# A planned two-part kernel: turns of x move to TensorE, folds stay in float32, and the order of work is planned in eight passes

## The chip, the cores and the metric

The kernel runs on one core of one Trainium2 chip. The metric is the device time of one launch in microseconds. Five engines work side by side: TensorE (PE, with its weight loads listed as PEld), VectorE (DVE), ScalarE (ACT), GpSimd (POOL, almost unused here) and SyncE (SP), which issues the DMAs.

## The reference

Three parts follow one another (B=8, H=8, S=512, 32 state rows, D=64; 4608 tokens in all).

```python
scores = scale * x @ state.T          # per batch and head: 512 x 32
xread  = softmax(scores) @ state      # 512 x 64
sread  = softmax(scores.T) @ x        # 32 x 64
x = concat([xread, sread])            # per batch 544 rows, 8 heads side by side: 512 columns
h = ((x @ w1) * (x @ w2)) @ w3        # w1, w2: 512 x 1024, w3: 1024 x 1024
x = h @ w_out                         # 1024 x 512
h = x @ w_in2                         # 512 x 2048
out = (h - tanh(h)) @ w_out2          # 2048 x 512
```

The weights arrive as 8-byte floats; x and state are 4-byte floats.

## The kernel before, in words

**Numbers.** A weight of 8 bytes is unpacked to float32 by five operations (`unpack_parts`): ACT takes the absolute value of the high word (L261), ACT or DVE scales the low word (L267, L269), DVE clamps (L278), shifts (L283) and joins (L289). For the fast matmul format (float32r) a float32 tile is split in a high and a low half: ACT copies (L220), DVE subtracts (L223), and each product is three matmuls (`PASSES`).

**First part, planned (everything up to `plan.run()`).**
- `w3_turn` turns a block of w3 by four 128x128 transposes on PE (tile `w_ps`, L242), ACT copies it out (`w3t`), and `w3_mul` multiplies it with w_out in float32 (tile `w3o_ps`, L735). There are 16 such turns with their products; the result takes the place of w3 and w_out.
- For each half of the batches (r = 0, 1) `turn_state` turns the state rows on PE (`u_ps`), they are split in halves (`uu`), and `fold` multiplies them with w1 and w2 (tile `m_ps`, L877; six matmuls on 64 rows, two at a time at different row positions). 32 folds go through PSUM and SBUF (`fe`) to DRAM (`mdr`). By them the read of the state and the product with w1 and w2 are one matmul per head.
- `attn_parts(b)`: x of a batch is loaded twice, as `xn` (for sread) and as `xb` (bands of 32 rows, eight DMAs of 128 KB, for the scores). DVE turns `xb` in 32x32 blocks (`xt`, L408, four per batch) and the state (`ut`). `scores` is 16 float32 matmuls on 32 rows and 32 columns (tile `sc_ps`, L421), each of which the trace shows as two records. Then come the two softmaxes, four transposes twice (`et_ps`), and `sread` (`sr_ps`, L516).
- `stage1(b, k, h)` makes the products with w1 and w2 (tile `ab_ps`, L250), `stage2` the product with the joined w3 (tile `y_ps`, L1027), for k = 0 to 7 in each of 9 blocks: 8 batches of 512 rows, and block B, the 256 state rows of all batches, which takes w1 and w2 themselves (tile `w`, split in halves at decode).
- w_in2 and w_out2 are decoded and stored to DRAM meanwhile.

**Second part, in a fixed order.** `stage3` (tile `h_ps`, L250), `curve`, `stage4` (tile `o_ps`, L1286) and `finish` for the 9 blocks.

**What sets the order of the first part.** Every operation is a `part` with an engine, a duration from a small cost table, what it needs, makes, takes and gives back. Parts lie in streams; each stream has a rank for each engine. `Plan.run` walks once: it takes the part that can start first and, among the parts of the same engine that can start within 250 ns of it, the one of the lowest rank. The order so found is the program order on each engine's queue. Four PSUM banks are shared by `ab`, `w3x`, `fold` and `ps` tiles, the others hold the accumulators. The turns of w3, their copies and the products `w3_mul` lie in one stream, one after the other.

## Time and profile before

| what | us |
|---|---|
| runs | 1343.75, 1333.1, 1341.79 (median 1341.79) |
| the profiled execution | 1337.37 |
| its span, first to last instruction | 1335.5 |
| PE busy in the span | 1282.8 (96%) |
| DVE busy | 978.2 (73%) |
| ACT busy | 723.9 (54%) |

Busy times are sums over an engine's instructions, overlaps counted once. The ends of matmuls are modelled, so PE's busy time holds part of its waits too. In the rows below a group of instructions shows its count as xN, then the busy time in us and the mean ns of one; a timeline row shows the start, the length from first start to last end, the engine, the line, and in brackets how long the engine stood idle before and what ended that.

### The profile page before, as it was taken

Reading aid. Unit: us, or ns where it says so; the run is one execution under the profiler, and the core shown is the slowest. Engines: PE = TensorE matmul, PEld = TensorE weight load, DVE = VectorE, ACT = ScalarE, POOL = GpSimd, SP = SyncE. Lnnn points to the kernel's source line nnn. Section 1 sums busy time; section 2 is a strip of 40 time slices with the busy share of each in tenths; the row PEclk is TensorE's granted clock in tenths of the full one; section 3 lists DMA queues with packets and bytes.
Section 4 is the critical chain, followed back from the end, with each engine's and each line's share of the span. In section 5 each row is a group of like instructions: output and inputs, shape, how many; then the busy total and the mean of one; then the engine's idle time right before and its main releaser. Section 6 shows DMA issues by size and latency. Waiting matters only on the chain.

```text
span 1335.5 us, 17513 instructions
## 1 busy us (share of the span) xinstructions
PE 1282.8 (96%) x6416; PEld 1005.6 (75%) x6416; DVE 978.2 (73%) x1638; ACT 723.9 (54%) x1172; POOL 0.7 (0%) x6
## 2 busy tenths in 40 slices
PE   6798999999999999999999999999999999999996
PEld 3345676767777689788888888888888888888886
DVE  7898786775655842559977687787876877768775
ACT  7788575564646622446555455454544545545454
POOL 0000000000000000000000000000000000000000
PEclk9999999999999999999999999999999999999999
DMA  9966887869899632722010010100101001001000
GB/s 326 270 226 212 255 256 214 246 200 280 250 250 284 189 91 95 220 69 90 1 64 1 9 56 0 64 0 1 64 0 54 10 1 64 1 0 48 1 32 16
DMA packets 98286, 150.58 MB, mean 113 GB/s; under 512 B 13976, under 2 KB 68248, under 8 KB 96152
## 3 DMA queue, kind: packets, MB, share of 16 engines
q1 hardware_dynamic: 98200, 149.46, 36.2%
q8 instruction: 51, 0.84, 0.3%
q14 instruction: 35, 0.29, 0.1%
HBM read 98.04 MB, written 51.38 MB: 112 GB/s over the span
## 4 chain that ended last, share of the span: by engine, by line
PE 73%; DMA 12%; DVE 5%; ACT 4%; SPq 4%; issue 1%; DVEq 0%; ACTq 0%
PE h_ps L250 26%; PE o_ps L1286 26%; PE ab_ps L250 9%; PE y_ps L1027 7%; DMA raw_w<-in_moe_w_in_dram 3%; DMA m<-mdr 2%; DMA raw_p<-in_moe_w_dram 2%; PE w3o_ps L735 2%; DMA raw_w<-in_moe_w_out_dram 1%; DMA mdr<-fe 1%; SPq L396 1%; SPq L974 1%; PE m_ps L877 1%; DMA raw_p<-in_moe_w_out_dram 1%; ACT raw L267 1%
## 5 line engine op out<-in xcount | busy, mean ns | idle before, releaser
L250 PE MATMUL h_ps<-yt,w2in 128*128 128x512 f32 (+1 forms) x1728 | 394.0, 377 | 0.0
L250 PEld LDWEIGHTS h_ps<-yt,w2in 128*128 128x128 f32 x1728 | 313.4, 188 | 61.1
L250 PE MATMUL ab_ps<-at,m 128*128 128x512 f32 x768 | 196.2, 404 | 14.1 <-ACT ac L220 4.2
L1027 PE MATMUL y_ps<-ph,w3o 128*128 128x512 f32 (+1 forms) x864 | 201.4, 381 | 3.0 <-ACT y L220 3.0
L250 PEld LDWEIGHTS ab_ps<-at,m 128*128 128x128 f32 x768 | 141.6, 191 | 60.0 <-ACT ac L220 13.9
L1027 PEld LDWEIGHTS y_ps<-ph,w3o 128*128 128x128 f32 x864 | 153.7, 188 | 39.4 <-issue 6.1
L223 DVE TENSOR_TENSOR ph<-ac,ph 128x512 fp32r<-128x512 f32 (+1 forms) x72 | 47.5, 660 | 85.8 <-ACT ph L220 84.8
L220 ACT ACTIVATE ph<-ac 128x512 fp32r<-128x512 f32 (+1 forms) x72 | 43.9, 610 | 104.6 <-PE y_ps L1027 91.7
L735 PE MATMUL w3o_ps<-wo,w3t 128*128 128x512 f32 x128 | 64.0, 646 | 12.6 <-ACT w3t L220 12.6
L735 PEld LDWEIGHTS w3o_ps<-wo,w3t 128*128 128x128 f32 x128 | 24.7, 203 | 43.0 <-issue 26.5
L1010 DVE TENSOR_TENSOR ac<-ab_ps,ac 128x512 f32<-128x512 f32 (+1 forms) x72 | 47.2, 655 | 4.7 <-PE ab_ps L250 4.5
L267 ACT ACTIVATE raw_w<-raw_w 128x512 uint16<-128x512 uint32 x32 | 43.6, 1362 | 0.6
L220 ACT ACTIVATE ac<-ab_ps 128x512 f32<-128x512 f32 (+1 forms) x72 | 40.4, 561 | 2.0 <-PE ab_ps L250 1.9
L1296 DVE COPY ob<-o_ps 128x512 f32<-128x512 f32 x17 | 11.8, 692 | 39.1 <-PE o_ps L1286 39.1
L261 ACT ACTIVATE dt_w<-raw_w 128x512 f32<-128x512 f32 x32 | 21.4, 668 | 32.0 <-DMA raw_w<-in_moe_w_in_dram 16.6
L223 DVE TENSOR_TENSOR m<-m 128x512 fp32r<-128x512 f32 x32 | 22.0, 688 | 22.3 <-ACT m L220 22.0
L220 ACT ACTIVATE fe<-m_ps 128x512 fp32r<-128x512 f32 (+1 forms) x48 | 28.1, 601 | 16.8 <-PE m_ps L877 7.6
L220 ACT ACTIVATE m<-m 128x512 fp32r<-128x512 f32 x32 | 20.2, 631 | 30.2 <-DMA m<-mdr 30.0
L220 ACT ACTIVATE ob<-o_ps 128x512 f32<-128x512 f32 x17 | 10.2, 599 | 45.0 <-PE o_ps L1286 45.0
L877 PE MATMUL m_ps<-w,uu 64*128 64x512 f32 x192 | 32.3, 427 | 2.0 <-DVE fe L900 1.2
L278 DVE TENSOR_SCALAR dt_w<-dt_w 128x512 f32<-128x512 f32 x32 | 13.4, 420 | 23.4 <-ACT dt_w L261 23.2
L877 PEld LDWEIGHTS m_ps<-w,uu 64*128 64x128 f32 x192 | 16.8, 184 | 16.8 <-issue 6.2
(1814 smaller groups left out, 2297.1 us busy)
## 6 DMA issues: line engine op xcount, KB each, us to landing
mdr<-fe SPq DMA_DIRECT2D x96, 256.0 KB, 3.2
m<-mdr SPq DMA_DIRECT2D x128, 128.0 KB, 4.6
xb<-in_x_dram SPq DMA_DIRECT2D x64, 128.0 KB, 3.6
raw<-in_moe_w_dram SPq DMA_DIRECT2D x16, 512.0 KB, 7.3
xn<-in_x_dram SPq DMA_DIRECT2D x8, 1024.0 KB, 6.4
m<-mdr SPq DMA_DIRECT2D x128, 64.0 KB, 2.7
raw_w<-in_moe_w_in_dram SPq DMA_DIRECT2D x16, 512.0 KB, 5.9
raw_w<-in_moe_w_out_dram SPq DMA_DIRECT2D x16, 512.0 KB, 5.5
```

The costliest lines, as they stand in the source:

```text
L220: nc.scalar.activation(dst, src, AF.Copy)
L223: nc.vector.tensor_tensor(out=lo, in0=src, in1=hi.bitcast(F32), op=ALU.subtract)
L250: nc.tensor.matmul(out_ap, lhs(i), rhs(j), start=(n == 0), stop=(n == m - 1))
L261: nc.scalar.activation(t.bitcast(F32), w[:, :, 1].bitcast(F32), AF.Abs)
L267: nc.scalar.activation(tail, w[:, :, 0], AF.Copy, scale=TAIL)
L278: nc.vector.tensor_scalar(out=t, in0=t, scalar1=EXP_LO, scalar2=EXP_HI, op0=ALU.max, op1=ALU.min)
L396: nc.sync.dma_start(xb[b][band(q, j), j].rearrange("p g c d -> p g (c d)"), x[b, 2 * q + j].rearrange("(g p c) d -> p g (c d)", p=NS, c=NC),)
L735: nc.tensor.matmul(acc[a], v[:, a * P:(a + 1) * P], wo[j][:, 512:].bitcast(F32), start=(j == 0), stop=(j == nj - 1),)
L877: nc.tensor.matmul(ts[j].rearrange("p (k f) -> p k f", k=2), uu[r][1][d, i, q * P:(q + 1) * P], w[d, :, l, q, :], start=(n == 0), stop=(n ...
L1010: nc.vector.tensor_tensor(out=ab[b, k], in0=ab[b, k, 1], in1=ab[b, k], op=ALU.mult)
L1027: nc.tensor.matmul(acc[o][:, :n], w3o[k // 4][:, k // 2 % 2, i, c + o * P:c + (o + 1) * P], p[:, j], start=(k == 0 and e == 0), stop=(k == ...
L1286: nc.tensor.matmul(acc[t], g[:, i, t * P:(t + 1) * P], w[:, l, c], start=(f == 0 and e == 0), stop=(f == NF - 1 and e == 2),)
```

## The change

- **x is loaded once and turned by PE.** `xb`, `load_xb`, the DVE transposes and the second copy of the state (`zb`, `ut`) are gone. `xn` is loaded by four DMAs of 256 KB with runs of 256 bytes, in two buffers. Four times per batch PE makes four 128x128 transposes (`turn_x`) and ACT copies the bank to `xt`.
- **Scores on 64 rows.** Eight float32 matmuls on 64 rows and 32 columns.
- **Float32 folds.** w1 and w2 are no longer split at decode: a block is unpacked in one piece of 1024 instead of two of 512, in place, and a fold is two float32 matmuls on 64 rows instead of six float32r ones. `uu` stays float32.
- **Late halves.** Block B takes its halves of w1 and w2 when it needs them (`own_hi` on ACT, `own_lo` on DVE), in the ring `m` that the other blocks' weights use.
- **Turns of w3 as an own stream**, ahead of the products in rank.
- **State rows row by row.** The columns of `xsr` go by row and batch, and so do the last two stores.
- **The plan is made eight times.** The first pass is the walk by ranks. After each pass `justify` goes backwards over the plan and finds for each part the latest start that would not move the end; these take the place of the ranks in the next pass. The pass with the earliest planned end of PE is kept.

```diff
             can = []
-            for s in self.streams:
+            for s, parts in zip(self.streams, lists):
                 seen = set()
-                for k, p in enumerate(s["parts"][:s["ahead"]]):
+                for k, p in enumerate(parts[:s["ahead"]]):
                     if p["eng"] not in seen:
                         seen.add(p["eng"])
                         t = self.start(p)
                         if t is not None:
-                            rank = s["rank"].get(p["eng"], 9) if p["rank"] is None else p["rank"]
-                            can.append((t, rank, s["parts"], k, p))
+                            can.append((t, p["late"], parts, k, p))
             if not can:
-                left = [s["parts"][0] for s in self.streams if s["parts"]]
+                left = [parts[0] for parts in lists if parts]
                 assert not left, [(p["eng"], p["need"], p["take"]) for p in left]
-                return
             t0, _, _, _, p0 = min(can, key=lambda c: c[0])
             t, _, parts, k, p = min(
                 (c for c in can if c[4]["eng"] == p0["eng"] and c[0] <= t0 + self.NEAR),
                 key=lambda c: (c[1], c[0]),
             )
             del parts[k]
-            self.emit(p, t)
+            self.place(p, t)
+            found.append(p)
+        return found
...
+    def justify(self, found):
+
+        end = max(p["span"][1] for p in found)
+        gaps = {e: [(0.0, end)] for e in self.REACH}
+        bound = {id(p): end for p in found}
+        for s in self.streams:
+            last = {}
+            for p in s["parts"]:
+                if p["eng"] in last:
+                    p["after"].append(last[p["eng"]])
+                last[p["eng"]] = p
+        late = {}
+        for p in sorted(found, key=lambda p: -p["span"][1]):
+            free = gaps[p["eng"]]
+            k = next(
+                (
+                    k for k in reversed(range(len(free)))
+                    if min(free[k][1], bound[id(p)]) - free[k][0] >= p["dur"]
+                ),
+                0,
+            )
+            a, b = free[k]
+            t = min(b, bound[id(p)]) - p["dur"]
+            free[k:k + 1] = [(a, t), (t + p["dur"], b)]
+            late[id(p)] = t
+            for q in p["after"]:
+                lag = q["lag"] if q["eng"] != p["eng"] or q["bytes"] else 0.0
+                bound[id(q)] = min(bound[id(q)], t - lag)
+        for p in found:
+            p["late"] = late[id(p)]
+
+    def run(self):
+        for s in self.streams:
+            for p in s["parts"]:
+                p["late"] = s["rank"].get(p["eng"], 9) if p["rank"] is None else p["rank"]
+        best = None
+        for _ in range(self.ROUNDS):
+            found = self.order()
+            end = max(p["span"][1] for p in found if p["eng"] == "PE")
+            if best is None or end < best[0]:
+                best = end, [(p, p["banks"]) for p in found]
+            self.justify(found)
+        for p, banks in best[1]:
+            self.picked += banks
+            p["fn"]()
...
-            uu[r] = (t, pt.tile([P, 2, 512], F32R, tag="uu", name=f"uu{r}"))
+            uu[r] = (t, pt.tile([P, 512], F32, tag="uu", name=f"uu{r}", bufs=2))
...
+                t = pt.tile([P, NC, H, D], F32, tag="xn", name=f"xn{b}", bufs=2)
+                xn[b] = t.rearrange("p c h d -> p c (h d)")
+                for c in range(NC):
+                    nc.sync.dma_start(
+                        t[:, c], x[b].rearrange("h (p c) d -> c p h d", c=NC)[c]
+                    )
...
-            def xt(j, e):
-                t = pt.tile([P, 512], F32, tag="xt", name=f"xt{b}_{j}{e}", bufs=4)
-                nc.vector.transpose(
-                    out=t.rearrange("p (c g i) -> p g c i", c=NC, g=4),
-                    in_=xb[b][:, j, :, :, e * NS:(e + 1) * NS],
-                )
-                s["xt", j, e] = t
+            def turn_x(q):
+                s["xp", q] = ps(f"x_ps{b}_{q}")
+                transposes(s["xp", q], [xn[b][:, c, q * P:(q + 1) * P] for c in range(NC)])
+
+            def xt(q):
+                s["xt", q] = pt.tile([P, 512], F32, tag="xt", name=f"xt{b}_{q}", bufs=4)
+                copy(s["xt", q], s["xp", q])
 
             def scores():
                 for j in range(G):
                     s["ps", j] = ps(f"sc_ps{b}_{j}")
-                for e in range(2):
-                    for q in range(KT):
-                        for j in range(G):
-                            d = band(q, j)
-                            nc.tensor.matmul(
-                                s["ps", j][q * NS:(q + 1) * NS],
-                                ut[b // 4][d, j, bb, e], s["xt", j, e][d],
-                                start=(e == 0), stop=(e == 1), tile_position=(d.start, q * NS),
-                            )
+                for q in range(KT):
+                    for j in range(G):
+                        d = slice(j * D, (j + 1) * D)
+                        c = q * P + bb * NS
+                        nc.tensor.matmul(
+                            s["ps", j][q * NS:(q + 1) * NS], uu[b // 4][1][d, c:c + NS],
+                            s["xt", q][d], start=True, stop=True, tile_position=(d.start, q * NS),
+                        )
...
-                    xsr[:, :, b * NS:(b + 1) * NS],
+                    xsr.rearrange("p q (n b) -> p q n b", b=B)[:, :, :, b],
...
+                    "PE", pe_t(4), turn_x, (q,), [("xn",)], [("xp", q)], [("ps", ("xp", q), 1)],
+                    [("xn",)],
+                )
+                p(
+                    "ACT", ("scalar", 512), xt, (q,), [("xp", q)], [("xt", q)],
+                    [("xt", ("xt", q), 1)], [("xp", q)],
                 )
             part(
-                a_s, "PE", 16 * 185, scores,
-                [("ut", b // 4)] + [(b, "xt", j, e) for j in range(G) for e in range(2)],
+                a_s, "PE", 1300, scores, [("uu", b // 4)] + [(b, "xt", q) for q in range(KT)],
...
+        t3_s = plan.stream({"PE": 2.8, "ACT": 1.5, "DVE": 1.5}, 40)
...
-                x_s, "PE", 4 * TURN, later(w3_turn, t), whole[:1], [("w3x", t)],
+                t3_s, "PE", 4 * TURN, later(w3_turn, t), whole[:1], [("w3x", t)],
...
-                x_s, "ACT", ("scalar", 512), lambda t=t: copy(w3v[t], w3x[t]),
+                t3_s, "ACT", ("scalar", 512), lambda t=t: copy(w3v[t], w3x[t]),
...
-        for kk in range(NK // 2):
-            for u in range(4):
-                k = 2 * kk + u // 2
-                unpack_parts(
-                    d_s, ("t12", kk, u), lambda kk=kk, u=u: raws["w12", kk][:, u // 2, u % 2],
-                    lambda kk=kk, u=u: w12_float(kk, u), 512, [("raw12", k, u % 2)],
-                    [("raw", ("t12", k), 4)] if u % 2 == 0 else (), (),
-                )
-            for u in range(4):
-                k = 2 * kk + u // 2
-                part(
-                    d_s, "ACT", ("scalar", 512), lambda kk=kk, u=u: copy(*w12_slice(kk, u)[1::-1]),
-                    [("t12", kk, v) for v in range(4)], [("h12", kk, u)], (), [("t12", k)],
-                )
-                part(
-                    d_s, "DVE", ("vector", 512), lambda kk=kk, u=u: low(*w12_slice(kk, u)),
-                    [("h12", kk, u)], [("w12", kk, u)], (), [("t12", k)],
-                )
+        for k in range(NK):
+            unpack_parts(
+                d_s, ("t12", k),
+                lambda k=k: raws["w12", k // 2][:, k % 2].rearrange("p h f -> p (h f)"),
+                lambda k=k: w12_float(k), 1024, [("raw12", k, h) for h in range(2)],
+                [("raw", ("t12", k))], [("t12", k)], end=lambda k=k: w12_whole(k),
+            )
...
-            w = w12[kk].rearrange("p k l (a f) -> p k l a f", a=KT)
+            w = w12_rows(kk)
             ts = fts[r, kk, q] = [ps(f"m_ps{r}_{kk}_{q}_{j}") for j in range(G)]
-            for n, (i, l) in enumerate(PASSES):
-                for j in range(G):
-                    d = slice(j * D, (j + 1) * D)
-                    nc.tensor.matmul(
-                        ts[j].rearrange("p (k f) -> p k f", k=2),
-                        uu[r][1][d, i, q * P:(q + 1) * P], w[d, :, l, q, :],
-                        start=(n == 0), stop=(n == len(PASSES) - 1), tile_position=(j * D, 0),
-                    )
+            for j in range(G):
+                d = slice(j * D, (j + 1) * D)
+                nc.tensor.matmul(
+                    ts[j].rearrange("p (k h f) -> p k h f", k=2, h=2),
+                    uu[r][1][d, q * P:(q + 1) * P], w[d, :, :, q],
+                    start=True, stop=True, tile_position=(j * D, 0),
+                )
...
+        def own_hi(k, h):
+            mt[B, k, h] = pa.tile([P, 2, 512], F32R, tag="m", name=f"m{B}_{k}{h}", bufs=3)
+            w = w12_rows(k // 2)[:, k % 2, h]
+            copy(mt[B, k, h][:, 0].rearrange("p (a f) -> p a f", a=KT), w)
+
+        def own_lo(k, h):
+            w = w12_rows(k // 2)[:, k % 2, h]
+            m = mt[B, k, h].rearrange("p l (a f) -> p l a f", a=KT)
+            low(w, m[:, 0], m[:, 1])
...
+                for h in range(2):
+                    part(
+                        m_s, "ACT", ("scalar", 512), later(own_hi, k, h),
+                        ["pa", ("s1", *steps[max(0, steps.index(z) - 2)], h)], [("mh", b, k, h)],
+                        [("m", ("m", b, k, h))],
+                    )
+                    part(
+                        m_s, "DVE", ("vector", 512), later(own_lo, k, h), [("mh", b, k, h)],
+                        [("m", b, k, h)],
+                    )
...
-                    ["pa"] + [
+                    ["pa"] + ([("mh", B, NK - 1, 1)] if b == B - 1 else []) + [
...
-                nb = P // NS
+
+                c = S + t * (P // B)
                 nc.sync.dma_start(
-                    out.rearrange("(b s) o -> b s o", b=B)[nb * t:nb * (t + 1), S:], ob[:, t]
+                    out.rearrange("(b s) o -> s b o", b=B)[c:c + P // B], ob[:, t]
```

## Rows read from the trace of the kernel before

**Rows 1.** The page, part 2: busy share of PE in 40 slices of the span, tenths.

```profile
PE   6798999999999999999999999999999999999996
```

**Rows 2.** Windows, busy us of each engine: the first part cut at 112; the second.

```profile
core 0: us, PE busy (x) PEld busy (x) DVE busy (x) ACT busy (x) POOL busy (x), PEclk, DMA share, GB/s
0.00:112.00 112.00, 89.52 (x400) 42.12 (x402) 93.94 (x159) 83.50 (x111) 0.70 (x6) 0.97 0.87 268
112.00:584.00 472.00, 451.83 (x2660) 346.65 (x2661) 298.76 (x559) 253.89 (x429) 0.00 (x0) 0.99 0.70 210
584.00:1335.00 751.00, 741.44 (x3359) 616.87 (x3357) 585.54 (x921) 386.50 (x634) 0.00 (x0) 1.00 0.08 28
```

**Rows 3.** Chain of waits, where the second part begins: start, length, what.

```profile
583.72 10.88 PE h_ps L250 x48
...
597.32 2.72 PE h_ps L250 x12
```

**Rows 4.** Groups on PE, 7 to 584 us; last column: idle before, and releasers.

```profile
L1027 PE MATMUL y_ps<-ph,w3o 128*128 128x512 f32 (+1 forms) x864 | 201.4, 381 | 3.0 <-ACT y L220 3.0
L250 PE MATMUL ab_ps<-at,m 128*128 128x512 f32 x768 | 196.2, 404 | 14.1 <-ACT ac L220 4.2 <-ACT fe L220 2.5 <-DMA raw_w<-in_moe_w_in_dram 1.8
L735 PE MATMUL w3o_ps<-wo,w3t 128*128 128x512 f32 x128 | 64.0, 646 | 12.6 <-ACT w3t L220 12.6
L877 PE MATMUL m_ps<-w,uu 64*128 64x512 f32 x192 | 32.3, 427 | 2.0 <-DVE fe L900 1.2 <-ACT fe L220 0.5 <-ACT w3t L220 0.3
L250 PE MATMUL ab_ps<-atsr,w 128*128 128x256 f32 x192 | 24.3, 284 | 0.1
L421 PE MATMUL sc_ps<-xt,ut 32*32 32x512 f32 x256 | 15.9, 593 | 0.0
L516 PE MATMUL sr_ps<-xn,e2t 128*32 128x64 f32 x512 | 10.1, 222 | 0.3 <-ACT ac L220 0.3
L242 PE MATMUL et_ps<-ident,sc 128*128 128x128 f32 x64 | 9.9, 278 | 1.5 <-ACT sc L446 1.5
```

**Rows 5.** Timeline of PE, the first turn of w3.

```profile
7.25 1.09 PE L242 MATMUL w_ps<-ident,wo 128*128 128x128 f32 x4 [7.25 <-DVE wo L289]
```

**Rows 6.** Timeline of PE, later turns and a product of w3.

```profile
33.65 0.60 PE L242 MATMUL w_ps<-ident,wo 128*128 128x128 f32 x4
34.08 0.60 PE L242 MATMUL u_ps<-ident,zst 128*128 128x128 f32 x4
35.21 3.70 PE L735 MATMUL w3o_ps<-wo,w3t 128*128 128x512 f32 x8 [0.53 <-ACT w3t L220]
38.75 0.60 PE L242 MATMUL w_ps<-ident,wo 128*128 128x128 f32 x4
```

**Rows 7.** Timeline of PE, one set of scores and a fold.

```profile
167.58 1.95 PE L421 MATMUL sc_ps<-xt,ut 32*32 32x512 f32 x32
169.45 0.96 PE L877 MATMUL m_ps<-w,uu 64*128 64x512 f32 x6
170.35 1.65 PE L1027 MATMUL y_ps<-ph,w3o 128*128 128x512 f32 x6
```

**Rows 8.** Groups on DVE, 0 to 112 us.

```profile
L223 DVE TENSOR_TENSOR w<-dt,w 128x512 fp32r<-128x512 f32 x12 | 8.0, 684 | 1.3 <-ACT w L220 1.3
...
L408 DVE STREAM_TRANSPOSE xt<-xb 128x512 f32<-128x512 f32 x8 | 5.3, 692 | 0.0
```

**Rows 9.** Groups on ACT, 0 to 112 us.

```profile
L220 ACT ACTIVATE w3t<-w_ps 128x512 f32<-128x512 f32 x16 | 9.8, 613 | 11.1 <-PE w_ps L242 11.0
```

**Rows 10.** DMA issues: count, KB each, median us to landing.

```profile
xb<-in_x_dram SPq DMA_DIRECT2D x64, 128.0 KB, 3.6
...
xn<-in_x_dram SPq DMA_DIRECT2D x8, 1024.0 KB, 6.4
...
zst<-in_state_dram SPq DMA_DIRECT2D x8, 64.0 KB, 8.4
```

More of the change, by code (lines that the diff above doesn't have):

```diff
@@ L50 @@
     REACH = {"PE": 200.0, "ACT": 130.0, "DVE": 130.0, "SP": 0.0}
+    ROUNDS = 8
     def __init__(self):
-        self.free = dict.fromkeys(self.REACH, 0.0)
-        self.moved = 0.0
-        self.made, self.slots, self.held, self.streams = {}, {}, {}, []
-        self.banks = [([0, 0.0], None) for _ in range(4)]
+        self.rings, self.streams = {}, []
         self.most = {"ab": 4, "w3x": 4, "fold": 2, "ps": 2}
@@ L67, in stream, with clear @@
         return s["parts"]
+    def clear(self):
+        self.free = dict.fromkeys(self.REACH, 0.0)
+        self.moved = 0.0
+        self.made, self.held = {}, {}
+        self.slots = {name: (n, []) for name, n in self.rings.items()}
+        self.banks = [([0, 0.0, []], None) for _ in range(4)]
     def start(self, p):
@@ L93, in start, with place @@
         return t
[L95 removed]
+    def place(self, p, t):
         end = t + p["dur"]
@@ L682, in unpack_parts @@
             part(
-                st, "DVE", ("vector", n), lambda: unpack_end(raw(), t()),
+                st, "DVE", ("vector", n), lambda: unpack_end(raw(), t(), end and end()),
                 [(key, "tail"), (key, "top")], [key], (), give,
@@ L913, in tile_kernel @@
                 f_s, "PE", 4 * TURN, later(turn_state, r), [("zst", r)], [("u_ps", r)],
-                [("fold", ("u_ps", r), 2), ("uu", ("uu", r), KT * NK // 2)], [("zst", r)],
+                [("fold", ("u_ps", r)), ("uu", ("uu", r), KT * NK // 2 + 4)], [("zst", r)],
             )
             part(
-                f_s, "ACT", ("scalar", 512), lambda r=r: copy(uu[r][1][:, 0], uu[r][0]),
-                [("u_ps", r)], [("uh", r)], (), [("u_ps", r)],
-            )
-            part(
-                f_s, "DVE", ("vector", 512),
-                lambda r=r: low(uu[r][0], uu[r][1][:, 0], uu[r][1][:, 1]),
-                [("uh", r)], [("uu", r)], (), [("u_ps", r)],
+                f_s, "ACT", ("scalar", 512), lambda r=r: copy(uu[r][1], uu[r][0]),
+                [("u_ps", r)], [("uu", r)], (), [("u_ps", r)],
             )
@@ L928, in tile_kernel @@
                     part(
-                        f_s, "PE", 6 * 177, later(fold, *f),
-                        [("uu", r)] + [("w12", kk, u) for u in range(4)], [("fold", *f)],
+                        f_s, "PE", 1080, later(fold, *f),
+                        [("uu", r)] + [("t12", 2 * kk + k) for k in range(2)], [("fold", *f)],
                         [("fold", ("m_ps", *f, j), 2 if r else 1) for j in range(G)], [("uu", r)],
@@ L961, in tile_kernel @@
         steps = [(b, k) for b in blocks for k in range(NK)]
-        m_s = plan.stream({"SP": 0})
+        m_s = plan.stream({"SP": 0, "ACT": 1, "DVE": 1})
         n_s = plan.stream({"ACT": 1, "DVE": 1})
@@ L1067, in tile_kernel @@
             else:
+                for h in range(2):
[8 more added lines that the diff above has]
+                    )
                 need = [(B - 1, "atsr", q) for q in range(0, KT, 2)]
-                need += [("w12", k // 2, u) for u in range(4)]
                 used, dur = [(B - 1, "atsr")], 12 * 120
@@ L1072, in tile_kernel @@
                 part(
-                    s1, "PE", dur, later(stage1, b, k, h), need, [("s1", *z, h)],
-                    [("ab", ("ab", *z, h))], used,
+                    s1, "PE", dur, later(stage1, b, k, h),
+                    need + ([("m", b, k, h)] if b == B else []), [("s1", *z, h)],
+                    [("ab", ("ab", *z, h))], used + ([("m", b, k, h)] if b == B else []),
                 )
```

134 lines of the change are left out of this document (44 added, 90 removed), and 3 rows, old and new, of the table plan.

## The prediction

> **What bounds the kernel now.** I read the slices first. PE is 90% busy or more from the fourth of 40 slices on [rows 1], so a gain has to come out of PE's work or of the time in which PE waits. Then the windows, cut where the kernel changes its nature: up to 112 us (w3 joined with w_out, decode, first attention), up to 584 us (stages 1 and 2), and the rest [rows 2]. The reader should see three things there. The second part holds 741 of 751 us of PE work at the full clock (1.00, so 2.4 GHz); nothing of the change touches it but the order of its last stores. Up to 112 us PE is busy for 89.5 us and DVE for 93.9, so DVE is the fuller engine. From 112 to 584 us PE is busy for 451.8 of 472 us and DVE for 298.8.
>
> Busy time hides waits, because ends of matmuls are modelled, so I also set up a floor for PE before 583.72 us, where the second part begins [rows 3]. Twelve matmuls of 512 columns take 2.72 us there back to back [rows 3]. By counts [rows 4]: 768 of `ab` and 768 of the 864 of `y` (96 are 256 wide) make 1536 x 2.72 / 12 = 348.2 us; the 192 + 96 narrow ones at 24.3 / 192 = 0.127 make 36.5; 16 products of w3 at 38.75 - 35.21 = 3.54 [rows 6] make 56.6; 32 folds at 170.35 - 169.45 = 0.90 and 8 sets of scores at 169.45 - 167.58 = 1.87 [rows 7] make 28.8 and 15.0; sread 10.1 [rows 4]; and some 36 groups of four transposes at 34.08 - 33.65 = 0.43 [rows 6] make 15.5. Together 510.7 us. PE starts at 7.25 us [rows 5] and has 576.5 us until 583.72, so **65.8 us are lost**. Shown as idle are 112 - 89.5 - 7.3 = 15.2 us early and 20.2 later [rows 2], of which 12.6 are products of w3 that wait for ACT's copy of their own turn [rows 4]. The granted clock of 0.97 and 0.99 is 0.03 x 112 + 0.01 x 472 = 8.1 us. The other 22.3 hide behind modelled ends.
>
> **The change part by part.**
>
> *PE's work grows.* Turns of x: 8 batches x 4 groups x 0.43 [rows 6] = +13.8 us. Scores: the 32 records that a set shows are four rounds, and half as many matmuls make two; (1.87 - 0.10) / 2 + 0.10 = 1.0 us, if 0.10 of a set is change-over, so 8 x 0.87 = -7.0. The ends are no gain at all and -8 x 0.94. Folds: six fast matmuls take 0.90 now. A float32 record of 512 columns takes 3.54 / 8 = 0.44 [rows 6]; two row halves that run side by side, as the eight tiles of the scores do [rows 7], take two rounds, 0.88, plus the 0.22 that 0.90 holds beyond three rounds of 0.227 (2.72 / 12): 1.10. 32 x 0.20 = +6.4. If the halves ran one after the other it would be 1.99, +35; the scores speak against it, since 32 records in 1.87 are far below 32 x 0.44. Sum: **+13.2 us**, all on the path, since PE is the engine that ends the first part.
>
> A turn's price has an upper end too: the record of one transpose is 0.278 us long [rows 4], and turns that do not overlap would cost 128 x 0.278 = 35.6 us. I take the spacing, 0.108, because it is that of transposes among float32 products. [...]
>
> *The turns of w3 run ahead.* When PE turns block t+1 before product t, the copy lies behind 3.54 us of product. The 12.6 us of waits [rows 4] go, if decode keeps the pace: -12.6. What is late next is DVE, at 93.9 of 112 us. In a stretch of 99.4 us that would be 94%. But the change takes from it 8.0 us of low halves of w and 5.3 of transposes [rows 8]; 80.6 of 99.4 is 81%, below the 84% it had. So the two edits hold only together, and I take the whole 12.6; the ends are 0 and 15.
>
> *ACT.* It loses 16 high halves of w in the decode, gains 32 copies of `xt`, and takes 16 halves again for block B. At 0.613 [rows 9] that is +19.6 us over 584, where ACT has 112 - 83.5 = 28.5 us free early and half of the rest [rows 2]. Up to 112 us it is 8 copies more and 12 less. I cost it at nothing. If PE had to wait for each copy of `xt`, it would be the wait that the products of w3 show, 0.53 [rows 6] or more, 32 times.
>
> *Late halves.* 16 subtractions at 0.684 [rows 8] move to where DVE is 63% busy [rows 2]: nothing. The loads of batch 7 now wait for the last copy of block B; everything that they need of `mdr` is stored by then, and PE has the products of block B beside them. Bounded by 0 and one landing of 128 KB, 3.6 us [rows 10]. I take 0.
>
> *Loads.* 64 issues of `xb` and the 16 of the second state go, and 8 of `xn` become 32; SP queues less. The pieces are runs of 256 bytes like the state rows'. The nearest rows are 6.4 us for a whole `xn` and 8.4 for 64 KB of state rows [rows 10], so a batch takes between 6.4 and 4 x 8.4 = 33.6 us. Two buffers and some 472 / 8 = 59 us per batch hide either. Only batch 0 has no load ahead of it, and products of w3 cover it; without that cover it is up to 27 us late. I take 0.
>
> *Eight passes.* What is left to gain is 65.8 - 12.6 = 53.2 us. The groups show of what kind it is: `ab` waits 14.1 us, with 4.2 for the copy of the previous `ab`, 2.5 for a copy of a fold and 1.8 for a decode's load [rows 4]. These are short operations that stood behind others on ACT and DVE, and an order by latest starts moves such things. It can move neither the clock's share directly nor what the plan does not know. The ends are 0 and all but the 8.1 of the clock. I take 40%, the shown idle (22.8) nearly whole and the hidden part not: **-21**.
>
> **The sum** against the profiled execution: 1337.4 + 13.2 - 12.6 - 21 = 1317. That execution lies 4.4 us under the median of the three runs, 1341.8, and above the fastest, 1333.1, so the median after may lie at 1317 to 1321; I say 1317.
>
> **The rivals.**
>
> *The plan closes nearly to the floor.* Losses fall from 65.8 to some 20: 1337.4 + 13.2 - 45.8 = 1305 or less. For it: no engine but PE is over 63% busy after 112 us. Against it: the plan works with fixed durations, and 22 us of loss are not even shown as waits. Chance 0.13.
>
> *The passes change nothing on the chip.* The walk by ranks stays the best pass, or what it plans is lost to loads that land late. Then +13.2 and -12.6 cancel: 1338. For it: DMA has a share of 0.87 and 0.70 [rows 2], which the plan models roughly. Chance 0.19.
>
> *Turns that do not overlap.* With all else as forecast, 128 x (0.278 - 0.108) = 21.8 us more [rows 4, 6]: 1339. Against it: every group of four in rows 6 is through in 0.43 us. Chance 0.02. [...]
>
> *Slower: PSUM banks.* A turn of x holds one of four shared banks from its first transpose until ACT has copied it, and no more than two such tiles may be held. Before, the transposes on DVE needed no bank at all. If `ab` then finds no free bank, or the third turn waits for the first copy, PE pays some 0.7 us (the wait before the products of w3, 0.53 [rows 6], and the modelled end) for each of the 32: 22 us, on top of the 13.2. Without any gain from the order: 1337.4 + 13.2 + 22 = 1373, and 1360 with the 12.6. It decides once ACT takes a copy later than PE has other work to put between. Against it: between 112 and 584 us ACT is 54% busy. Chance 0.09.
>
> *The forecast*, 1305 to 1328: chance 0.57.
>
> **How the numbers follow.** Within 1% of the median, about what a measurement of this kernel can tell from no change, is 1328 to 1355. The forecast and the first rival are faster (0.70), the passes without effect and the turns without overlap are the same (0.21), the banks slower (0.09). The range leaves out half of the first rival and the banks: 1299 to 1343. The others lie in it.
>
> **What would show it.** Right: no wait of `w3o_ps` for `w3t` beyond some 2 us; the first `h_ps` at 555 to 570 us; scores at 1.0 and folds at 1.1 us; DVE clearly under 84% up to the first `ab`; the second part 751 us as now. Wrong: `ab_ps` or transposes waiting for ACT's copies of `xt`; folds near 2 us; the clock under 0.97 where x is turned; a first `h_ps` at 580 or later.

## The result and the profile after

The changed kernel takes **1320.66 us** (median of six runs, 1318.77 to 1324.37) against 1338.35 for the kernel before in the same comparison: ratio 0.9873, 95% interval 0.9851 to 0.9895. The forecast was 1317 in a range of 1299 to 1343. The profiled execution took 1320.41 us, its span is 1318.2.

The PE row of the page, part 2, of the changed kernel, hardly different from [rows 1] at this grain (the last slice is 8 for 6):

```profile
PE   6898999999999999999999999999999999999998
```

Next the windows of the changed kernel, cut where its second part begins (columns as in [rows 2]):

```profile
core 0: us, PE busy (x) PEld busy (x) DVE busy (x) ACT busy (x) POOL busy (x), PEclk, DMA share, GB/s
0.00:112.00 112.00, 94.99 (x431) 46.28 (x433) 85.92 (x136) 85.26 (x105) 0.70 (x6) 0.98 0.87 263
112.00:571.50 459.50, 451.07 (x2564) 347.67 (x2565) 283.22 (x521) 267.15 (x450) 0.00 (x0) 1.00 0.67 198
571.50:1318.00 746.50, 741.88 (x3361) 617.31 (x3359) 585.67 (x921) 386.77 (x635) 0.00 (x0) 1.00 0.08 29
```

Against [rows 2]: up to 112 us DVE is lighter (93.94 to 85.92) and PE fuller (89.52 to 94.99). In the second part PE's work is the same (741.44 and 741.88). The chain of waits of the changed kernel gives the border, for [rows 3]:

```profile
571.63 10.88 PE h_ps L313 x48
...
585.24 2.72 PE h_ps L313 x12
```

The second part begins 12.1 us earlier (583.72 to 571.63) and takes 5.2 us less after that (1335.5 - 583.7 = 751.8, 1318.2 - 571.6 = 746.6). The groups on PE up to 572 us, for [rows 4] (lines have moved: L250 is now L313, L1027 L1038, L735 L755, L877 L885, L421 L453, L242 L305, L220 L283):

```profile
L313 PE MATMUL ab_ps<-at,m 128*128 128x512 f32 x768 | 194.8, 400 | 6.7 <-DMA m<-mdr 2.5 <-ACT e2t L283 2.0 <-DVE fe L286 1.0
L1038 PE MATMUL y_ps<-ph,w3o 128*128 128x512 f32 x768 | 189.4, 394 | 0.3 <-ACT y L283 0.3
L755 PE MATMUL w3o_ps<-wo,w3t 128*128 128x512 f32 x128 | 62.2, 634 | 1.5 <-ACT w3t L283 1.5
L885 PE MATMUL m_ps<-raw,uu 64*128 64x512 f32 x128 | 37.0, 641 | 3.9 <-issue 3.9
L313 PE MATMUL ab_ps<-atsr,m 128*128 128x256 f32 x192 | 23.5, 283 | 1.5 <-ACT atsr L283 1.1 <-DVE atsr L286 0.3
L305 PE MATMUL x_ps<-ident,xn 128*128 128x128 f32 x128 | 17.6, 274 | 0.1
...
L453 PE MATMUL sc_ps<-xt,uu 64*32 64x512 f32 x128 | 10.1, 601 | 1.4 <-ACT ac L283 1.4
```

The products of w3 wait 1.5 us for ACT where they waited 12.6, `ab` waits 6.7 for 14.1, `y` 0.3 for 3.0. In return folds (3.9), scores (1.4) and block B (1.5) now wait a little. The timeline of PE of the changed kernel shows the new operations, for [rows 6, 7] (start, length, and idle before in brackets):

```profile
38.19 0.60 PE L305 MATMUL u_ps<-ident,zst 128*128 128x128 f32 x4
38.63 0.60 PE L305 MATMUL w_ps<-ident,wo 128*128 128x128 f32 x4
...
43.38 1.47 PE L305 MATMUL x_ps<-ident,xn 128*128 128x128 f32 x12
44.69 0.60 PE L305 MATMUL w_ps<-ident,dt_p 128*128 128x128 f32 x4
45.12 0.60 PE L305 MATMUL x_ps<-ident,xn 128*128 128x128 f32 x4
45.56 3.60 PE L755 MATMUL w3o_ps<-wo,w3t 128*128 128x512 f32 x8
...
85.76 1.13 PE L885 MATMUL m_ps<-raw,uu 64*128 64x512 f32 x4
86.82 1.09 PE L453 MATMUL sc_ps<-xt,uu 64*32 64x512 f32 x16
87.84 1.13 PE L885 MATMUL m_ps<-raw,uu 64*128 64x512 f32 x4
```

A group of four turns of x is through in 0.44 us (45.12 to 45.56), a fold in 1.06 (85.76 to 86.82), a set of scores in 1.02 (86.82 to 87.84). The 128 turns together, start to next start, hold 14.1 us of PE. A set of scores took 1.88 us before (the median of eight sets; [rows 7] show one at 1.87).

**Where the time came from.** PE's work before the second part grew by 14.1 - 8 x (1.88 - 1.02) + 32 x (1.06 - 0.90) = 12.3 us, so the floor, what PE's work would take back to back, is 510.7 + 12.3 = 523.0. PE begins at 7.32, and 571.63 - 7.32 - 523.0 = 41.3 us are lost, where 65.8 were. +12.3 - 24.5 is, to 0.1 us, the 12.1 us by which the second part begins earlier; 5.2 more come at its end. Of the 24.5, e2 (below) shows 11.0 to be the work of the eight passes: with one pass the second part begins at 582.6, so 582.6 - 7.3 - 523.0 = 52.3 us are lost, 13.5 less than before the change.

### The profile page after: what moved, and what is told of

Same layout as the page of the kernel before. It is cut to its first block, busy times and chain, and to the rows that moved or that the text cites. A ratio compares the mean times of both kernels' runs of the same rounds, so it can differ in the third digit from the quotient of the medians.

```text
span 1318.2 us, 17291 instructions
## 1 busy us (share of the span) xinstructions
PE 1287.9 (98%) x6352; PEld 1011.3 (77%) x6352; DVE 954.8 (72%) x1578; ACT 739.2 (56%) x1188; POOL 0.7 (0%) x6
## 4 chain that ended last, share of the span: by engine, by line
PE 84%; DMA 6%; DVE 5%; ACT 2%; SPq 1%; issue 1%; DVEq 0%; ACTq 0%
PE h_ps L313 27%; PE o_ps L1307 26%; PE ab_ps L313 11%; PE y_ps L1038 11%; PE w3o_ps L755 4%; PE m_ps L885 2%; DMA w2lin<-w2dr_in 1%; DMA ydr<-y 1%; PE x_ps L305 1%; DMA w2dr_out<-dt_w 1%; DMA m<-mdr 1%; DMA raw_p<-in_moe_w_out_dram 1%; SPq L977 1%; PE sc_ps L453 1%; DMA raw_w<-in_moe_w_out_dram 0%
## 5 line engine op out<-in xcount | busy, mean ns | idle before, releaser
L313 PE MATMUL h_ps<-yt,w2in 128*128 128x512 f32 (+1 forms) x1728 | 394.0, 377 | 0.0
L313 PEld LDWEIGHTS h_ps<-yt,w2in 128*128 128x128 f32 x1728 | 313.4, 188 | 61.1
L1038 PE MATMUL y_ps<-ph,w3o 128*128 128x512 f32 (+1 forms) x864 | 201.7, 382 | 0.3 <-ACT y L283 0.3
L313 PE MATMUL ab_ps<-at,m 128*128 128x512 f32 x768 | 194.8, 400 | 6.7 <-DMA m<-mdr 2.5
L1038 PEld LDWEIGHTS y_ps<-ph,w3o 128*128 128x128 f32 x864 | 153.9, 188 | 39.3 <-issue 8.7
L313 PEld LDWEIGHTS ab_ps<-at,m 128*128 128x128 f32 x768 | 141.3, 189 | 51.0 <-ACT ac L283 5.8
L283 ACT ACTIVATE ph<-ac 128x512 fp32r<-128x512 f32 (+1 forms) x72 | 44.1, 612 | 80.3 <-PE y_ps L1038 72.9
L755 PE MATMUL w3o_ps<-wo,w3t 128*128 128x512 f32 x128 | 62.2, 634 | 1.5 <-ACT w3t L283 1.5
L1021 DVE TENSOR_TENSOR ac<-ab_ps,ac 128x512 f32<-128x512 f32 (+1 forms) x72 | 47.2, 656 | 13.3 <-PE ab_ps L313 12.1
L755 PEld LDWEIGHTS w3o_ps<-wo,w3t 128*128 128x128 f32 x128 | 24.8, 203 | 32.6 <-issue 28.8
L283 ACT ACTIVATE ac<-ab_ps 128x512 f32<-128x512 f32 (+1 forms) x72 | 40.4, 561 | 6.0 <-PE ab_ps L313 6.0
L885 PE MATMUL m_ps<-raw,uu 64*128 64x512 f32 x128 | 37.0, 641 | 3.9 <-issue 3.9
L283 ACT ACTIVATE fe<-m_ps 128x512 fp32r<-128x512 f32 (+1 forms) x48 | 28.4, 606 | 16.1 <-PE m_ps L885 8.9
L324 ACT ACTIVATE dt_w<-raw_w 128x512 f32<-128x512 f32 x32 | 21.4, 667 | 28.0 <-DMA w2dr_out<-dt_w 12.1
L283 ACT ACTIVATE ob<-o_ps 128x512 f32<-128x512 f32 x17 | 10.2, 599 | 45.1 <-PE o_ps L1307 45.1
L341 DVE TENSOR_SCALAR dt_w<-dt_w 128x512 f32<-128x512 f32 x32 | 13.5, 421 | 22.5 <-ACT dt_w L324 22.5
L286 DVE TENSOR_TENSOR fe<-m_ps,fe 128x512 fp32r<-128x512 f32 x32 | 21.2, 685 | 7.6 <-DMA mdr<-fe 5.6
L283 ACT ACTIVATE m<-m 128x512 fp32r<-128x512 f32 x32 | 20.2, 635 | 11.3 <-DMA m<-mdr 11.1
```

The costliest lines, as they stand in the source:

```text
L283: nc.scalar.activation(dst, src, AF.Copy)
L286: nc.vector.tensor_tensor(out=lo, in0=src, in1=hi.bitcast(F32), op=ALU.subtract)
L313: nc.tensor.matmul(out_ap, lhs(i), rhs(j), start=(n == 0), stop=(n == m - 1))
L324: nc.scalar.activation(t.bitcast(F32), w[:, :, 1].bitcast(F32), AF.Abs)
L341: nc.vector.tensor_scalar(out=t, in0=t, scalar1=EXP_LO, scalar2=EXP_HI, op0=ALU.max, op1=ALU.min)
L755: nc.tensor.matmul(acc[a], v[:, a * P:(a + 1) * P], wo[j][:, 512:].bitcast(F32), start=(j == 0), stop=(j == nj - 1),)
```

## The experiments

Each kernel was compared with the kernel before. "Begins" is where the first `h_ps` stands in the chain of waits of the one profiled run; a smaller number means a shorter first part. The kernel before and e1 differ in the first part only in the columns that a few small copies write, and their profiled runs begin 3.1 us apart, so a difference of some 3 us in this column alone says little.

| run | ratio to before (95%) | median, us | second part begins |
|---|---|---|---|
| kernel before | 1 | | 583.7 |
| changed kernel | 0.9873 (0.9851 to 0.9895) | 1320.66 | 571.6 |
| e1 before + rows | 0.9971 (0.9953 to 0.9989) | 1333.71 | 580.6 |
| e2 one pass | 0.9939 (0.9916 to 0.9963) | 1330.98 | 582.6 |
| e3 w3 one stream | 0.9891 (0.9872 to 0.9910) | 1323.74 | 574.4 |
| e4 split at decode | 1.0044 (1.0026 to 1.0063) | 1344.79 | 595.0 |
| e5 NEAR 30 | 0.9824 (0.9787 to 0.9861) | 1314.29 | 567.7 |
| e6 x on DVE | 0.9870 (0.9831 to 0.9909) | 1319.49 | 570.9 |
| e7 halves early too | 0.9999 (0.9976 to 1.0022) | 1337.36 | 590.5 |
| e8 decode and rows | 1.0088 (1.0059 to 1.0117) | 1347.37 | 596.8 |
| e9 ring of three | 0.9876 (0.9848 to 0.9904) | 1319.83 | 574.1 |
| e10 own stream on before | 1.0037 (1.0013 to 1.0060) | 1341.71 | 587.9 |
| e11 NEAR 0 | 0.9824 (0.9792 to 0.9855) | 1313.04 | 562.8 |
| e12 NEAR 30, one pass | 1.0003 (0.9980 to 1.0026) | 1338.01 | 586.6 |

### e1: the kernel before with row-wise state rows

```diff
-                    xsr[:, :, b * NS:(b + 1) * NS],
+                    xsr.rearrange("p q (n b) -> p q n b", b=B)[:, :, :, b],
...
-                    out.rearrange("(b s) o -> b s o", b=B)[nb * t:nb * (t + 1), S:], ob[:, t]
+                    out.rearrange("(b s) o -> s b o", b=B)[c:c + P // B], ob[:, t]
```

> The kernel before with one edit: the columns of xsr by row and batch, and so the last two stores. In the two traces the last stores keep SP waiting 7.4 us before and 2.3 us after, and the second part is 751.8 against 746.7 us long. If the stores' pattern is the cause, this kernel takes 1338.4 - 5.1 = 1333 us, with the first part unchanged at about 584 us and the last wait near 2.3 us. If the shorter last wait of the changed kernel comes from something else (the load on the DMA engines at that moment, or the earlier end), it stays at 1338 us.

The last wait of SP, for the last store, in the kernel before, and then in e1 (us in total, times, longest):

```profile
SPq L1363 <- DMA out_dram<-ob: 7.5, 1, 7.5
```

```profile
SPq L1363 <- DMA out_dram<-ob: 2.4, 1, 2.4
```

The changed kernel shows 2.4 there as well. So the last store is 5.1 us shorter with the second part's work untouched: in e1's profiled run it takes 1327.2 - 580.6 = 746.6 us, where it took 751.8. The time fell by 0.29% of 1338 = 3.9 us (by the interval 1.5 to 6.3), as the first expectation had it. While the two stores run, the mean busy share of the 16 DMA engines is 0.24 in the kernel before (1327 to 1334 us) and 0.71 in the changed kernel (1314.5 to 1317). The prediction named "the order of its last stores" and gave it no price.

### e2: one pass by ranks

```diff
-    ROUNDS = 8
+    ROUNDS = 1
```

> The changed kernel with one pass of planning instead of eight: the walk by ranks alone. The prediction gave the eight passes 21 us; if that holds, 1320.7 + 21 = 1342 us, with the waits of ab_ps for ACT back at about 14 us. If the gain of the first part comes from the lighter decode and from the early turns of w3, the passes are worth little: 1321 to 1325 us.

10.3 us by the medians, 8.8 by the ratios (0.9939 - 0.9873), 11.0 by where the second part begins: between the two expectations. The prediction had 21. The waits of `ab` are 10.0 us, where 14 were expected. The windows of e2, and then of the changed kernel, say where:

```profile
0.00:112.00 112.00, 97.42 (x413) 48.66 (x413) 86.57 (x131) 87.71 (x104) 0.70 (x6) 1.00 0.83 256
112.00:560.00 448.00, 430.47 (x2485) 328.19 (x2481) 273.59 (x515) 256.31 (x437) 0.00 (x0) 0.99 0.69 200
```

```profile
112.00:560.00 448.00, 439.57 (x2513) 338.15 (x2514) 282.50 (x520) 264.81 (x446) 0.00 (x0) 1.00 0.69 202
```

Up to 112 us the walk by ranks keeps PE fuller than the eight passes do (97.42 against 94.99). What the passes give comes after it: 439.57 against 430.47 us in the same 448.

### e3: turns of w3 in one stream with the products

```diff
-                t3_s, "PE", 4 * TURN, later(w3_turn, t), whole[:1], [("w3x", t)],
+                x_s, "PE", 4 * TURN, later(w3_turn, t), whole[:1], [("w3x", t)],
...
-                t3_s, "ACT", ("scalar", 512), lambda t=t: copy(w3v[t], w3x[t]),
+                x_s, "ACT", ("scalar", 512), lambda t=t: copy(w3v[t], w3x[t]),
```

> The changed kernel with the turns of w3 back in the stream of their products, eight passes kept. If the early turns are what took the wait of w3o_ps for w3t from 12.6 to 1.5 us, and nothing else can use that time, the wait returns and the time is 1320.7 + 11 = 1332 us. If PE fills those waits with folds and turns of x under the new plan, or decode sets the pace there, it stays at 1321 to 1324 us.

Groups on PE of e3 up to the second part:

```profile
L313 PE MATMUL ab_ps<-at,m 128*128 128x512 f32 x768 | 193.6, 400 | 5.5 <-ACT m L283 2.3 <-DMA m<-mdr 1.9 <-ACT ac L283 1.0
...
L755 PE MATMUL w3o_ps<-wo,w3t 128*128 128x512 f32 x128 | 61.9, 629 | 6.9 <-ACT w3t L283 6.7
```

The wait for `w3t` is back at 6.7 us, but only 3 us of time come with it, and the intervals of the two ratios overlap: the second expectation. That the passes order the rest around the late turns is the likely reason; it was not tested.

### e4: the decode, the folds and the halves of the kernel before

```diff
-        for k in range(NK):
-            unpack_parts(
-                d_s, ("t12", k),
...
+            for u in range(4):
+                part(
+                    d_s, "ACT", ("scalar", 512), lambda kk=kk, u=u: copy(*w12_slice(kk, u)[1::-1]),
...
+                part(
+                    d_s, "DVE", ("vector", 512), lambda kk=kk, u=u: low(*w12_slice(kk, u)),
```

Everything else is as in the changed kernel, except that `ph` has three buffers for want of room (e9 is the control) and the state's halves for the folds (`uh`) have one, as in the kernel before.

> The changed kernel with the decode of w1 and w2 as before (two pieces of 512, halves made at once, six float32r matmuls per fold, block B from the ready halves); the ring ph has three tiles again, for lack of room. PE's work falls by 32 x (1.06 - 0.90) = 5 us, DVE gets 8 us more before 112 us. If the lighter decode is the condition of the shorter first part, the time rises by 8 to 15 us, to 1329 to 1336. If PE's work is what counts, it falls to 1316.

24 us slower than the changed kernel, more than the 8 to 15 expected, and slower than the kernel before. The window up to 112 us of e4, and a line of its timeline:

```profile
0.00:112.00 112.00, 87.36 (x365) 44.59 (x365) 85.06 (x143) 85.02 (x113) 0.70 (x6) 0.92 0.81 247
```

```profile
99.81 2.10 PE L897 MATMUL m_ps<-w,uh 64*128 64x512 f32 x6 [3.29 <-DVE fe L920]
```

PE is at 87.36 of 112 us with a granted clock of 0.92. The loss lies late in this stretch: from 80 to 112 us PE is busy for 20.70 us at 0.72, where the changed kernel has 29.99 at 1.00. Up to 112 us folds wait 6.7 us for DVE's copies of earlier folds (`fe`); in the changed kernel none does. The halves in the decode bring these waits, but not simply by filling DVE: the copy that ends the 3.29 us above stood idle for 1.51 us itself, until the store of an earlier `fe` to DRAM had given a buffer back. By which engine or store the folds fall behind was not tested.

### e5: a smaller window for choosing by deadline

```diff
-    NEAR = 250.0
+    NEAR = 30.0
```

> The changed kernel with a window of 30 ns instead of 250 in which the planner may prefer a part with an earlier latest start over the part that could start first. The one-pass kernel showed the order to be worth 10 us. If PE's remaining waits come from parts that were preferred although they start later, they shrink further: 1311 to 1316 us. If the plan's last microseconds are lost on the chip to loads and to copies that end late, 1319 to 1323 us.

The chain of waits of e5:

```profile
551.39 16.32 PE y_ps L1038 x72
567.71 10.88 PE h_ps L313 x48
```

1314.29 us, 0.9824 of the kernel before, as the first expectation had it; the second part begins 3.9 us earlier than in the changed kernel.

### e6: x loaded twice and turned by DVE, scores on 32 rows

The diff gives back `load_xb`, `turn_heads`, the DVE transposes and the 16 matmuls of a set of scores, as in the kernel before; its core:

```diff
-            def turn_x(q):
...
+                nc.vector.transpose(
+                    out=t.rearrange("p (c g i) -> p g c i", c=NC, g=4),
```

> The changed kernel with x loaded twice and turned by DVE, and 32-row scores, as before the change (ring ph three tiles for lack of room); all else kept. PE's work falls by 128 turns x 0.110 - 8 x (1.87 - 1.02) = 7 us, DVE's grows by 32 x 0.69 = 22 us. If PE's work sets the end, 1314 us. If DVE's relief is what shortened the first part, 1328 to 1335 us.

No difference: 1319.49 us, between the two expectations. The window up to 112 us of e6, and a line of its timeline:

```profile
0.00:112.00 112.00, 94.17 (x433) 45.19 (x434) 91.31 (x144) 82.13 (x99) 0.70 (x6) 0.95 0.91 280
```

```profile
55.01 1.11 PE L305 MATMUL et_ps<-ident,sc 128*128 128x128 f32 x4 [6.25 <-ACT sc L509]
```

Without the turns PE has 14.1 - 6.9 = 7.2 us less to do, a floor of 515.8 us. The second part begins at 570.9 and PE at 7.4, so 47.7 us are lost, 6.4 more than in the changed kernel, and the two nearly cancel. What shows of the loss is DVE at 91.31 of 112 us again, a granted clock of 0.95, and the first softmax, for which PE waits 6.25 us; which of these costs how much was not tested.

### e7: the halves in the decode as well

```diff
+                part(
+                    d_s, "ACT", ("scalar", 512), later(early_hi, k, h), [("t12", k)],
...
+                part(
+                    d_s, "DVE", ("vector", 512), later(early_lo, k, h), [("eh", k, h)],
```

The added 16 copies on ACT and 16 subtractions on DVE write tiles that nothing reads; `ph` has three buffers here too.

> The changed kernel with 16 more copies on ACT and 16 more subtractions on DVE in the decode of w1 and w2, into a tile that nothing reads (the halves as before the change; folds stay float32 and wait for none of them; ring ph three tiles for room). If the work of the halves early on is what cost 24 us in the kernel that splits at decode, the time is 1332 to 1343 us. If it was that the folds waited for the halves, or the six-matmul folds, it stays at 1321 to 1326 us.

The window up to 112 us of e7, and lines of its timeline:

```profile
0.00:112.00 112.00, 89.56 (x402) 44.09 (x403) 87.75 (x137) 86.66 (x107) 0.70 (x6) 0.94 0.83 251
```

```profile
102.47 3.78 PE L906 MATMUL m_ps<-raw,uu 64*128 64x512 f32 x6 [4.39 <-DVE fe L929]
...
111.42 1.22 PE L906 MATMUL m_ps<-raw,uu 64*128 64x512 f32 x1 [3.11 <-DVE fe L929]
```

17 us slower than the changed kernel, as the first expectation had it: the same waits as in e4 (7.5 us of the folds for `fe` up to 112 us; from 80 to 112 PE is busy for 22.15 us at a granted clock of 0.79), made by the dead work alone. So early halves cost much even where no fold needs them. What share of e4's 24 us this is can't be read from it, since e7 makes the halves twice, early and again for block B.

### e8: the lighter decode and the rows, without the rest

The kernel of e6 with one pass by ranks and the turns of w3 in the stream of the products (the edits of e2 and e3).

> The kernel before with two parts of the change: decode of w1 and w2 in pieces of 1024 with float32 folds and late halves, and the stores by row (one pass by ranks, turns of w3 in the stream of their products, x on DVE). If the lighter decode alone shortens the first part, 1338 - 5 - 10 = 1320 to 1325 us. If it helps only together with a new order or with x on PE, 1331 to 1335 us.

The timeline of PE in e8:

```profile
111.17 3.70 PE L802 MATMUL w3o_ps<-wo,w3t 128*128 128x512 f32 x8
114.81 1.13 PE L932 MATMUL m_ps<-raw,uu 64*128 64x512 f32 x4
...
117.97 3.69 PE L802 MATMUL w3o_ps<-wo,w3t 128*128 128x512 f32 x8
128.84 6.54 PE L313 MATMUL ab_ps<-at,m 128*128 128x512 f32 x16 [7.18 <-ACT m L283]
```

SP's and ACT's side of that wait in the same timeline:

```profile
123.84 5.47 SPq L1024 DMA_DIRECT2D m<-mdr  x12
128.16 0.63 ACT L283 ACTIVATE m<-m 128x512 fp32r<-128x512 f32 x1 [5.86 <-DMA m<-mdr]
```

Slower than the kernel before by 0.88%. By ranks, products of w3 run until 121.7 us, and the first `ab` then waits 7.18 us for `m`. ACT had waited 5.86 us itself, for the loads of the first folds (`m<-mdr`), which SP issued from 123.84 us on. So the lighter decode is worth nothing without the rest of the change, and the time is above both expectations. e2 also has one pass by ranks and lies 1.5% lower; it differs from e8 by the own stream of w3's turns, x on PE and the fourth buffer of `ph`. Which of these does it was not tried.

### e9: three buffers of `ph`

```diff
-            ph[b, k] = pa.tile([P, 2, 512], F32R, tag="ph", name=f"ph{b}_{k}", bufs=4)[:, :, :n]
+            ph[b, k] = pa.tile([P, 2, 512], F32R, tag="ph", name=f"ph{b}_{k}", bufs=3)[:, :, :n]
```

> The changed kernel, but with three buffers of ph in place of four, as the runs e4, e6 and e7 had to have for want of room. Theory: the ring is not what made e4 and e7 slow, so this is within 3 us of the changed kernel (1318 to 1324, ratio 0.985 to 0.990). Rival: the fourth buffer carries a good part of the 24 and 17 us, then 1326 or more.

1319.83 us: three buffers, which the kernel before has as well, cost nothing by themselves, and the ring does not explain e4 and e7.

### e10: turns of w3 as an own stream, on the kernel before

```diff
+        t3_s = plan.stream({"PE": 2.8, "ACT": 1.5, "DVE": 1.5}, 40)
...
-                x_s, "PE", 4 * TURN, later(w3_turn, t), whole[:1], [("w3x", t)],
+                t3_s, "PE", 4 * TURN, later(w3_turn, t), whole[:1], [("w3x", t)],
...
-                x_s, "ACT", ("scalar", 512), lambda t=t: copy(w3v[t], w3x[t]),
+                t3_s, "ACT", ("scalar", 512), lambda t=t: copy(w3v[t], w3x[t]),
```

> The kernel before, with one thing done alone: the turns of w3 and their copies in a stream of their own. Theory (early turns need the lighter decode or the planned order): the waits of the products of w3 for ACT shrink from 12.6 us, but other waits of the early stretch take their place, and the time is that of before within 6 us (1333 to 1344). Rival (the prediction's step, -12.6 us by itself): 1326, ratio 0.990 or less.

Groups on PE of e10 up to 566 us:

```profile
L736 PE MATMUL w3o_ps<-wo,w3t 128*128 128x512 f32 x128 | 61.7, 625 | 3.0 <-ACT w3t L220 2.4 <-DVE w3o L223 0.5
L878 PE MATMUL m_ps<-w,uu 64*128 64x512 f32 x192 | 35.4, 452 | 11.9 <-DVE fe L901 4.7 <-ACT fe L220 3.4 <-ACT w L220 1.5
```

The waits for `w3t` fall from 12.6 to 2.4 us, as the prediction had it, and the waits of the folds rise from 2.0 to 11.9. The time does not fall; it rises by 0.37%, as the theory had it.

### e11: no window at all

```diff
-    NEAR = 250.0
+    NEAR = 0.0
```

> The changed kernel with NEAR = 0 in place of 250: on each engine the part that can start first is always taken, late starts only break ties. Theory (a small window keeps PE from waiting for parts that are late by plan): as with NEAR = 30, 1311 to 1318. Rival (NEAR = 30 was one lucky order among many, and with 0 the deadlines have no say): 1320 or more.

The window of 50 to 62 us in e11, then three windows of the changed kernel in the same stretch, and two lines of its timeline:

```profile
50.00:62.00 12.00, 10.77 (x42) 5.34 (x34) 11.20 (x21) 11.97 (x17) 0.00 (x0) 1.00 1.00 244
```

```profile
50.00:54.00 4.00, 1.15 (x16) 0.14 (x4) 2.11 (x4) 3.97 (x5) 0.00 (x0) 1.00 1.15 294
54.00:57.00 3.00, 1.97 (x5) 0.83 (x6) 3.00 (x5) 2.80 (x7) 0.00 (x0) 0.82 1.03 277
57.00:60.00 3.00, 3.00 (x6) 1.21 (x5) 2.93 (x7) 2.95 (x4) 0.00 (x0) 0.61 0.65 217
```

```profile
53.70 1.23 DVE L354 SCALAR_TENSOR_TENSOR raw<-raw,dt 128x1024 uint32<-128x1024 uint32 x1 [1.08 <-ACT raw L330]
...
55.03 1.24 PE L885 MATMUL m_ps<-raw,uu 64*128 64x512 f32 x4 [3.87 <-issue]
```

1313.04 us, the same ratio as e5, 0.9824. The rival had expected the deadlines to lose their say. They keep it, because parts that have been ready for some time can all start at the moment their engine comes free, and among those the latest start still chooses. With 250 an engine may also be held for a part that is not ready yet. In the changed kernel PE stands idle for 3.87 us before the first fold at 55.03. The profile names no releaser for it, but DVE's join of the fold's weights (`raw`) ends at 53.70 + 1.23 = 54.93. That wait, and the lower clock behind it, are not in e11, where products of w3 stand on PE at this point and PE is busy for 10.77 of these 12 us (8.13 in the changed kernel). That the window made this wait is not shown: a single choice can hold an engine by no more than 250 ns.

### e12: the small window with one pass

> The changed kernel with NEAR = 30 and one pass by ranks in place of eight. Theory: the window and the passes are worth about 6 and 10 us each by themselves, so one pass with the small window lies at 1320 to 1328. Rival (the small window alone does it, the passes add nothing to it): 1312 to 1318. Third: the window pays only where late starts are used, then 1329 to 1333, as with one pass and 250.

The edits are those of e2 and e5 together. Its windows, and then the first window of e5:

```profile
0.00:112.00 112.00, 87.68 (x402) 42.74 (x403) 85.03 (x132) 86.42 (x104) 0.70 (x6) 0.98 0.80 244
112.00:560.00 448.00, 434.87 (x2481) 333.68 (x2480) 271.75 (x512) 255.61 (x433) 0.00 (x0) 0.99 0.69 201
```

```profile
0.00:112.00 112.00, 97.17 (x482) 48.67 (x482) 90.97 (x147) 89.73 (x111) 0.70 (x6) 1.00 0.86 259
```

All three expectations missed: 1338.01 us, slower than each of them. The small window by ranks costs 7 us (1330.98 to 1338.01), and with it the passes are worth 24 (1338.01 to 1314.29). Window and passes are no separate terms.

## Why the prediction was right, and where its steps were not

The forecast case came true: faster by 1.3%, 1320.7 for 1317, the second part beginning at 571.6 (forecast 555 to 570, missed by 1.6). Step by step:

| step | predicted, us | found, us |
|---|---|---|
| turns of x | +13.8 | +14.1 |
| scores | -7.0 | -6.9 |
| folds | +6.4 | +5.1 |
| lost time of PE | -33.6 (12.6 + 21) | -24.5 |
| last stores | 0 | -5.1 |
| sum | -20.4 | -17.3 (span) |

- **PE's work** came out to a microsecond (12.3 for 13.2), because each price was taken from start to next start and not from the length of a record. The records of the turns are 274 ns long, and 128 of them hold 14.1 us, not 35. The Trainium skill (TensorE: Matmul & The Clock Gate, Part 4, PE-mode transpose) gives about 275 ns for a transpose in a kernel. By it the sum would have been an estimated 128 x (0.275 - 0.108) = 21 us higher; the trace agrees with it as the length of a record and not as the time that the engine is taken. The granted clock was 1.00 (2.4 GHz) in each stretch behind 112 us where turns of x lie, such as 131.9 to 139.5 us.
- **Early turns** were the step with a condition, and the condition decided. The waits for `w3t` shrink wherever the turns have their own stream (1.5 us here, 2.4 in e10, 4.1 at most, in e12). The 12.6 us do not follow from that alone: on the kernel before the stream alone gave none of it (e10), and taking it out of the changed kernel cost 3 (e3). The prediction's words "the two edits hold only together" were right: with both and without the eight passes (e2) 13.5 us less are lost than before. As a gain of the early turns alone the 12.6 does not hold.
- **The lighter decode**, which the prediction had as DVE's relief and as a condition only, is the part that carries most under the planned order. Putting the 16 halves back into the decode as dead work costs 17 us, and the whole old decode 24 (e7, e4). Both put copies on ACT back as well as subtractions on DVE, so that it is DVE's relief is not shown. DVE's busy time does not tell it: up to 112 us it is 85.92 here (77%, below the 84% it had), 87.75 in e7 and 85.06 in e4, and with 91.31 e6 is no slower. The decode is no term of its own either: without the planned order, the early turns and x on PE it makes the kernel slower (e8).
- **The turns of x and the loads** were costed at nothing beyond PE's work, and that held: turns wait 0.1 us and no `ab` waits for `xt`. What the prediction didn't ask is whether they are needed: in sum with the scores they cost PE 7.2 us and e6, which has not got them, loses about as much elsewhere and is as fast.
- **The eight passes** were mis-sized: 21 for about 9 to 11 (e2). The prediction took the shown idle nearly whole. It fell from 35.4 to 18.1 us (112 - 94.99 - 7.3 = 9.7 early and 8.4 up to 571.5), about half. The clock's share fell from 8.1 to some 4: 0.02 x 112 = 2.2, and 1.7 for the 28 us from 112 to 140 us at 0.94, which the rounded mean of 1.00 hides. The part behind modelled ends hardly changed, 22.3 to about 19. With a window of 30 the passes are worth 24 us over one pass with the same window (e12, e5).
- **The second part** was held to be untouched. Its work is, but its last store is 5.1 us shorter (e1). That the total came so near is in part luck: this made up for half of what the passes fell short. Without it the time would be 1320.7 + 5.1 = 1325.8, still within the forecast's 1305 to 1328.

Of the rivals, the passes without effect is refuted by e2 and e12, turns that don't overlap by the 14.1 us, and banks by the 0.1 us. The plan near the floor (1305) wasn't reached, but e11, at 1313, went half the way.

**The better kernel.** NEAR = 0 and NEAR = 30 give 0.9824 of the kernel before each, in two comparisons, 0.5% under the changed kernel's 0.9873; their intervals still touch its interval. The gain has a place in the trace, up to 62 us, but only part of it: the second part begins 8.8 us earlier in e11, and PE's shown idle up to 112 us differs by 1.5, the clock's share there by some 2 (0.98 and 1.00), and the busy time from 112 to 560 us by 3.3 (442.86 for 439.57). **Open** remains how much of a few microseconds between any two plans is mechanism and how much is the order that happened to come out. Each edit of the planner's input changes the whole order, so the 3 us of e3 and the 1 us of e6 are not to be read as prices. The passes were not tried alone on the kernel before.

## What to carry to other kernels

Price an added or removed PE operation by the spacing from its start to the next start beside the neighbours it will have. When an order is planned, don't add the gains of edits that share an engine: here a lighter decode without the other edits and an own stream alone made the kernel slower, a small window made one pass slower, and the whole change with the passes and the small window gave 1.8%. Look at the last transfer of the program even where the work ahead of it is untouched.
